# Attention, soft mixture of experts and MLP on one core: RoPE's last additions of pairs 1 to 5 as accumulating transfers from GpSimd's queue, with a new order of the first pairs

## The chip, the core and the metric

The kernel runs on one core of a Trainium2 chip. The core has a matmul engine (TensorE, PE in the rows), VectorE (DVE), ScalarE (ACT), GpSimd (POOL) and SyncE (SP), each with a queue of its own that it works off in order, and 16 DMA engines that all queues share. The metric is the device time of one execution in microseconds. The kernel before takes 566.4 us, the median of three runs (566.14 to 568.69).

## What is computed

The reference has three stages, all in float32:

- Attention over 4 batches of 8 heads, 576 positions, head size 64. Queries and keys are first rotated (RoPE): with the halves x1, x2 of a head's 64 numbers, the result is x1·cos - x2·sin and x1·sin + x2·cos. Then come the scores (scaled by 1/8), their softmax and the product with the values.
- A soft mixture of experts on the 2304 tokens of width 512: logits against `phi` (32 slots), a softmax over tokens that mixes tokens into slots, 8 experts of 4 slots each with a hidden width of 1024 and ReLU, and a softmax over slots that mixes the experts' results back into tokens.
- An MLP from 512 to 2048 and back, with the squared ReLU between.

```
q_rot, k_rot = (rotate(q), rotate(k))
scores = scale * np.matmul(q_rot, k_rot.transpose(0, 1, 3, 2))
attn = np.exp(scores - max);  attn = attn / (sum + 1e-09)
out = np.matmul(attn, v)
```

The host lays out the inputs. For each pair of heads it gives one array `qk[p]` of 128 rows (two heads of 64) by four planes of 576 columns: keys, queries, keys with their halves swapped, queries with their halves swapped. With that, RoPE is plain arithmetic on whole rows: plane · cos + swapped plane · (signed) sin.

## The kernel before

**The work in pairs.** The 32 heads are worked off as 16 pairs, 0 to 15. A pair passes through these steps (the function names are those of the listing):

- `load` brings the four planes into one of two buffers, `raws[p % 2]`, 1152 KB, from SyncE's queue. From pair 4 on a load is cut into three pieces. A buffer can be loaded again once `parts_pair` of the pair that held it is through.
- `rope_pair` computes in place, for each half t (0: keys, 1: queries): plane t times cos (d = 0), plane t + 2 times sin (d = 1), and the addition of the second to the first (d = 2). Each is one operation on 128 x 576 numbers. For pair 0 it runs on VectorE, for all other pairs on GpSimd (L543, a helper line that all of them share).
- `parts_pair` splits each rotated plane into a high part, rounded to the matmul's format by ScalarE (L577), and a low part, the difference, by GpSimd (L543 again, into tLa or tLb). Three products of high and low parts replace one exact product.
- `windows` copies the last 64 columns of the parts on ScalarE.
- `max_unit` computes scores from the high parts alone on TensorE (L654) and takes row maxima on VectorE (L665), nine units a pair (four blocks of 128 keys for each of two query halves, and one unit, called BOTH, for the keys left over, for both query halves together). `max_rows` turns the maxima into rows, which two small transfers (L703, 2.5 KB each) carry to where `st_unit` reads them.
- `st_unit` computes the scores (L738, six matmuls) less the maxima (L745, two matmuls) into one of three pairs of score banks, ScalarE takes the exponential (L758), and GpSimd adds the first two blocks of a half into one partial sum (L766; in the last two pairs also further blocks, L771, listed by `folded`).
- `pv_unit` multiplies with the values (L789; L784 for BOTH). `norm` sums the exponentials with matmuls against ones (L813) and scales on VectorE. `logits` (L863, L868) and transposes (L886) pass the result on; after every fourth pair `slots_in` mixes the tokens into slots (L931, L969).

Filler matmuls (L1880) stand where the plan expects TensorE to wait.

**The order.** The kernel doesn't run these functions in their order. `Plan.op` records each operation with its engine, what it reads and writes, and a rank; `emit` then lays them out one after the other, always the one of lowest rank among those that can start soonest by the plan's estimates of durations. The ranks stand in the table `ORDER`, by function and engine: the first number in a row is the first operation of that kind recorded, and so on through the pairs. In `("rope_pair", "POOL", None)` of the kernel before, six numbers belong to a pair: 35, 41, 49 are the two multiplications and the addition of pair 1's keys, 45, 54, 68 those of its queries. In `("parts_pair", ...)` two numbers belong to a pair, in `("max_unit", ...)` and `("st_unit", ...)` nine, in the order of `SEQ`: four blocks of the first query half, BOTH, four of the second; in `("st_unit", "POOL", None)` two partial sums a pair. Ranks of one table can be compared across engines: a lower rank is planned earlier. Each engine then takes its own operations strictly in the order of emission, and semaphores hold one back until what it reads is there.

The place of the change is `rope_pair`:

```
(0, a, a, None, ALU.mult, tk[0], ka),
(1, b, b, None, ALU.mult, tk[1], kb),
(2, a, a, b, ALU.add, kb, ka),
```

In `norm`, the matmuls against ones write four quarters of 32 rows, so that up to four run beside each other; pairs of quarters are added later on VectorE. With four operands (the partial sum, blocks 2 and 3, BOTH) or two, all quarters are in use. Only the last pair's second half has three.

**After attention** the expert weights (`free`, L1174) are loaded into the buffers that attention has left, then the experts and the MLP run, the MLP's second product at L1806.

Of the kernel before, what the change touches and what calls it, by code (L numbers as in the profile page):

```python
# [15 lines left out]
ALU = mybir.AluOpType  # L16
# [22 lines left out]
class Plan:  # L39
# [23 lines left out]
            11, 12, 15, 13, 16, 18  # L63
# [5 lines left out]
            17, 19, 55, 79, 117, 150, 194, 224, 273, 305, 346, 361, 429, 454, 526, 531, 631, 633, 721, 724, 815, 818, 910, 914, 1013, 1015, 1101, 1104, 1193,  # L69
            1196, 1261, 1268  # L70
        ),
        ("parts_pair", "POOL", None): (
            22, 28, 60, 86, 124, 160, 199, 230, 279, 314, 359, 369, 435, 460, 532, 543, 637, 648, 732, 742, 825, 836, 922, 929, 1023, 1032, 1112, 1120, 1202,
            1210, 1273, 1281
        ),
        ("rope_pair", "POOL", None): (
# [4 lines left out]
        ),  # L81
        ("load", "SP", None): (
            36, 99, 173, 176, 180, 237, 240, 242, 322, 323, 327, 373, 377, 379, 468, 471, 473, 557, 561, 565, 659, 662, 665, 753, 755, 758, 846, 849, 852, 942,
            946, 949, 1043, 1045, 1047, 1131, 1133, 1136
        ),
        ("windows", "ACT", None): (
            23, 30, 82, 81, 156, 132, 226, 217, 309, 296, 406, 408, 499, 502, 606, 608, 698, 701, 791, 794, 884, 887, 988, 990, 1078, 1081, 1168, 1171, 1265,
            1275, 1331, 1332
        ),
# [7 lines left out]
        ),  # L97
        ("max_unit", "DVE", None): (
# [13 lines left out]
        ),  # L112
        ("max_rows", "SP", None): (
            51, 62, 134, 136, 219, 222, 312, 317, 415, 417, 509, 510, 615, 618, 707, 710, 800, 803, 893, 896, 997, 1000, 1087, 1090, 1177, 1180, 1270, 1274, 1358,
            1355, 1422, 1418
        ),
        ("max_rows", "ACT", None): (
            52, 63
# [1853 lines left out]
```

## Time and profile before

| | |
|---|---|
| median of three runs | 566.4 us |
| the profiled execution's own time | 565.09 us |
| its span, first to last instruction | 563.3 us |
| TensorE busy | 544.0 us (97%) |
| VectorE busy | 398.6 us (71%) |
| ScalarE busy | 295.7 us (52%) |
| GpSimd busy | 229.9 us (41%) |
| granted TensorE clock | 1.0 throughout |
| read from and written to device memory | 77.92 and 6.82 MB |

The profile comes from one execution under the hardware profiler. Times in it count from the first instruction. The attention stage lasts until about 294 us, the experts until about 335, the MLP to the end. A share of busy time is a mean over these stages: GpSimd's 41% is near 100% in the first 110 us and nothing after attention. Busy times of TensorE include overlapping matmuls, whose ends are modelled, so its work is better read from how far apart the starts of equal units lie. In a timeline row, the brackets give the time the engine stood idle before the row, and what ended it.

### The profile page before, as it was taken

To read this page: it belongs to the slowest core of one execution; us is meant where nothing else is said; L and a number is where in the kernel's file an instruction comes from. 1 tells how busy PE (TensorE), PEld (TensorE's weight loads), DVE (VectorE), ACT (ScalarE), POOL (GpSimd) and SP (SyncE) were. 2 spreads that over 40 slices of the span, in tenths; PEclk is the share of its full clock that TensorE was granted. 3 is DMA by queue.
4 is the path that set the end of the run, shared out by engine and by line. 5 is a ranking of instruction groups with operands and counts; after the bars stand their busy time and mean duration, and the time that the engine had idled before them with its cause. 6 is when DMAs were issued, how large, how long until landed. Compare 5 with 4: busy or idle time off the path is not lost.

```text
span 563.3 us, 13271 instructions
## 1 busy us (share of the span) xinstructions
PE 544.0 (97%) x5406; PEld 416.7 (74%) x5406; DVE 398.6 (71%) x878; ACT 295.7 (52%) x568; POOL 229.9 (41%) x178
## 2 busy tenths in 40 slices
PE   4999999999999999999999999999999999999996
PEld 3656666566665666666642258999999999999996
DVE  6587788888897887876468748965775595554553
ACT  2334545664555655544426548975944564354440
POOL 4999999988889788723610000000000000000000
PEclk9999999999999999999999999999999999999999
DMA  7447796877784357222989997132200220000333
GB/s 237 139 132 184 167 249 188 221 192 195 210 219 117 93 144 201 100 99 101 338 295 396 409 401 255 39 111 76 76 1 1 76 76 2 1 1 1 113 113 112
DMA packets 37741, 85.68 MB, mean 152 GB/s; under 512 B 12176, under 2 KB 12848, under 8 KB 36528
## 3 DMA queue, kind: packets, MB, share of 16 engines
q1 hardware_dynamic: 37398, 84.24, 48.3%
q8 instruction: 42, 0.69, 0.5%
q10 hardware_dynamic: 282, 0.59, 0.4%
q14 instruction: 19, 0.16, 0.1%
HBM read 77.92 MB, written 6.82 MB: 150 GB/s over the span
## 4 chain that ended last, share of the span: by engine, by line
PE 81%; DMA 9%; DVE 5%; POOL 2%; ACT 1%; issue 1%; SPq 0%; DVEq 0%
PE bank L1806 35%; PE bank L738 11%; PE obank L789 11%; PE bank L654 5%; PE bank L813 5%; PE bank L745 3%; PE obank L1736 3%; DVE mcol L665 2%; DMA w__1345<-in_w_dram 2%; DMA tEb<-in_w_dram 2%; DMA tLb<-in_w_in_dram 2%; PE obank L784 2%; PE bank L886 2%; DMA ident<-in_ident_dram 1%; POOL arena L543 1%; DMA w__448<-in_w_dram 1%
## 5 line engine op out<-in xcount | busy, mean ns | idle before, releaser
L758 ACT ACTIVATE tO<-bank 128x576 f32<-128x576 f32 x140 | 84.2, 650 | 84.4 <-PE bank L745 83.3
L665 DVE TENSOR_REDUCE mcol<-bank 128x2 f32<-128x576 f32 x144 | 103.2, 749 | 22.6 <-PE bank L654 13.1
L543 POOL TENSOR_TENSOR arena<-arena 128x576 f32<-128x576 f32 x78 | 111.0, 1444 | 8.8 <-DMA arena<-in_qk_dram 8.0
L1806 PE MATMUL bank<-w,tEb 128*128 128x256 f32 x864 | 106.5, 279 | 0.1
L1806 PEld LDWEIGHTS bank<-w,tEb 128*128 128x128 f32 x864 | 103.5, 188 | 2.4 <-issue 1.6
L789 PE MATMUL obank<-tO,pb 128*64 128x288 f32 x496 | 74.8, 419 | 0.0
L766 POOL TENSOR_TENSOR pb<-tO 128x576 f32<-128x576 f32 x30 | 42.9, 1430 | 31.0 <-ACT tO L758 29.4
L1806 PE MATMUL bank<-w,tEa 128*128 128x256 f32 x432 | 53.0, 278 | 0.0
L1806 PEld LDWEIGHTS bank<-w,tEa 128*128 128x128 f32 x432 | 51.6, 188 | 1.2 <-issue 1.2
L1806 PE MATMUL bank<-w,tO 128*128 128x256 f32 x432 | 51.6, 277 | 0.0
L1806 PEld LDWEIGHTS bank<-w,tO 128*128 128x128 f32 x432 | 51.1, 188 | 0.0
L789 PEld LDWEIGHTS obank<-tO,pb 128*64 128x64 f32 x496 | 29.8, 136 | 22.7 <-issue 9.3
L1747 ACT ACTIVATE pb<-obank 128x384 f32<-128x384 f32 x47 | 21.7, 495 | 36.8 <-PE obank L1736 36.8
L1747 ACT ACTIVATE w__1091<-obank 128x384 f32<-128x384 f32 x48 | 21.8, 491 | 36.5 <-PE obank L1736 36.2
L654 PEld LDWEIGHTS bank<-tEb 64*128 64x128 f32 x180 | 16.3, 184 | 21.5 <-DVE mcol L665 4.4
L813 PE MATMUL bank<-tO,ones 128*32 128x288 f32 x224 | 31.9, 409 | 0.0
L654 PE MATMUL bank<-tEb 64*128 64x288 f32 x180 | 30.5, 355 | 0.7 <-DVE mcol L665 0.5
L819 DVE STREAM_TRANSPOSE bank<-bank 128x288 f32<-128x288 f32 x32 | 15.9, 496 | 19.2 <-PE bank L813 15.8
L543 POOL TENSOR_TENSOR tLb<-arena,tEb 128x576 fp32r<-128x576 f32 x20 | 28.6, 1448 | 1.3 <-ACT tEb L577 1.3
L738 PE MATMUL bank<-tEb 64*128 64x288 f32 x180 | 28.5, 313 | 0.3 <-DVE mcol L665 0.2
L1736 PE MATMUL obank<-x,tO 128*128 128x384 f32 x95 | 26.8, 336 | 0.5 <-DVE tO L1664 0.5
L738 PE MATMUL bank<-tLb,tEb 64*128 64x288 f32 x180 | 26.6, 292 | 0.0
(299 smaller groups left out, 1095.2 us busy)
## 6 DMA issues: line engine op xcount, KB each, us to landing
arena<-in_qk_dram SPq DMA_DIRECT2D x14, 576.0 KB
arena<-in_qk_dram SPq DMA_DIRECT2D x12, 512.0 KB
arena<-in_w_dram SPq DMA_DIRECT2D x8, 512.0 KB
pb<-in_v_dram SPq DMA_DIRECT2D x12, 320.0 KB
arena<-in_qk_dram SPq DMA_DIRECT2D x3, 1152.0 KB
tLb<-in_w_in_dram SPq DMA_DIRECT2D x3, 1024.0 KB
pb<-in_w_in_dram SPq DMA_DIRECT2D x3, 1024.0 KB
w__448<-in_w_dram SPq DMA_DIRECT2D x4, 512.0 KB
```

The costliest lines, as they stand in the source:

```text
L543: ENG[e].tensor_tensor(out=o, in0=x, in1=y, op=how)
L654: nc.tensor.matmul(on_ring(tok)[:, j, 0:HQ], lhsT=x[rows], rhs=hi[rows, 0, HALF[c]], start=(u < BOTH or c == 0), stop=(u < BOTH or c == 1),)
L665: lambda e: nc.vector.tensor_reduce(out=mcol[:, h, :, u], in_=on_ring(tok)[:, :, 0:HQ], op=ALU.max, axis=AX.X),
L738: nc.tensor.matmul(st[:, j, 0:HQ], lhsT=w[rows], rhs=q[y][rows, HALF[c]], start=(i == 0 and (u < BOTH or c == 0)), stop=False,)
L745: nc.tensor.matmul(st[:, j, 0:HQ], lhsT=pick[rows, w : w + 128], rhs=mrow[rows, HALF[c]], start=False, stop=(u < BOTH or c == 1),)
L758: lambda e: nc.scalar.activation(out=pr, in_=on_ring(tok)[:, :, 0:HQ], func=AF.Exp, scale=0.125),
L766: lambda e: nc.gpsimd.tensor_tensor(out=acc, in0=one, in1=pr, op=ALU.add),
L789: nc.tensor.matmul(BANKS[6 + h][o, 0:HQ], lhsT=vr[:, u, j, :], rhs=pr[:, j, :], start=(h == 0 and u == 0), stop=(h == 1 and u == 3))
L813: nc.tensor.matmul(sm[QUAD[2 * j + w], 0:HQ], lhsT=one, rhs=x[:, j, :], start=(i == 0), stop=(i + w + 2 > last))
L1736: lambda e, i=i, t0=t0: nc.tensor.matmul(BANKS[i][:, 0:384], lhsT=wst_of()[:, 128 * fc : 128 * fc + 128], rhs=cst_of()[:, t0 : t0 + 384], ...
L1747: lambda e, i=i, h=h: nc.scalar.activation(out=rg_of()[:, 0, h], in_=BANKS[i][:, 0:384], func=AF.Relu),
L1806: nc.tensor.matmul(BANKS[c][:, cols], lhsT=gt[:, x, 128 * c : 128 * c + 128], rhs=wo[:, fc % 2, y, cols], start=(fc % FQ == 0 and i == 0 a ...
```

## The change

- For pairs 1 to 5 (`MOVED`) `rope_pair` records only the two multiplications of each half. One operation follows them: a DMA issued from GpSimd's queue that reads planes 2 and 3 of the buffer and adds them to planes 0 and 1 in place (`accum_op=ALU.add`), for keys and queries at once: 128 rows of 1152 numbers, 590 KB. Ten additions go and five DMAs come. Its rank is the fifth number of a pair in `("rope_pair", "POOL", None)`.
- The ranks of pairs 0 to 5 are new on all engines. From about pair 6 on, each rank is the old one less 5, so the order there is the same.
- In pair 0 (VectorE) the addition of the first half goes behind the second multiplication of the second half.
- `folded` reads a table `FOLDED` in place of its condition. `norm` spreads an odd last operand over two quarters, half of the columns each.

```
         ("rope_pair", "DVE", None): (
-            11, 12, 15, 13, 16, 18
+            11, 12, 16, 13, 15, 17
...
         ("parts_pair", "ACT", None): (
-            17, 19, 55, 79, 117, 150, 194, 224, 273, 305, 346, 361, 429, 454, 526, 531, 631, 633, 721, 724, 815, 818, 910, 914, 1013, 1015, 1101, 1104, 1193,
...
+            18, 19, 82, 79, 130, 134, 220, 216, 273, 279, 377, 372, 429, 436, 519, 532, 625, 628, 716, 719, 810, 813, 905, 909, 1008, 1010, 1096, 1099, 1188,
...
         ("parts_pair", "POOL", None): (
-            22, 28, 60, 86, 124, 160, 199, 230, 279, 314, 359, 369, 435, 460, 532, 543, 637, 648, 732, 742, 825, 836, 922, 929, 1023, 1032, 1112, 1120, 1202,
...
+            21, 28, 112, 101, 135, 141, 250, 238, 280, 286, 398, 391, 435, 440, 549, 538, 634, 646, 727, 737, 820, 831, 917, 924, 1018, 1027, 1107, 1115, 1197,
...
         ("rope_pair", "POOL", None): (
-            35, 41, 49, 45, 54, 68, 76, 96, 110, 116, 131, 143, 149, 171, 186, 193, 207, 214, 236, 244, 262, 250, 285, 295, 290, 304, 330, 336, 341, 352, 381,
...
+            45, 49, 35, 40, 54, 76, 92, 60, 68, 109, 158, 166, 150, 175, 187, 199, 205, 213, 219, 244, 314, 335, 320, 326, 343, 355, 365, 380, 348, 405, 416, 454,
...
         ("max_unit", "PE", "r"): (
-            21, 24, 25, 29, 32, 34, 38, 40, 42, 92, 94, 103, 84, 85, 100, 107, 111, 113, 162, 175, 185, 165, 167, 182, 189, 192, 196, 227, 243, 269, 229, 241,
-            265, 277, 278, 286, 310, 340, 360, 324, 326, 355, 365, 375, 385, 372, 432, 450, 400, 419, 446, 456, 466, 478, 464, 529, 551, 493, 513, 542, 560, 576,
...
+            25, 22, 32, 24, 38, 29, 34, 41, 43, 107, 87, 93, 113, 118, 116, 106, 102, 96, 145, 143, 206, 182, 155, 189, 168, 193, 197, 235, 255, 308, 233, 237,
+            274, 266, 272, 245, 291, 283, 347, 374, 337, 336, 371, 367, 316, 385, 389, 388, 379, 421, 426, 485, 472, 483, 482, 516, 498, 442, 520, 471, 554, 570,
...
         ("st_unit", "PE", "r"): (
-            64, 61, 70, 67, 77, 121, 115, 119, 125, 154, 151, 187, 178, 197, 206, 200, 203, 209, 257, 251, 276, 261, 288, 307, 292, 303, 337, 348, 345, 362, 351,
...
+            58, 66, 71, 63, 110, 119, 81, 84, 99, 172, 179, 164, 177, 159, 198, 190, 201, 203, 252, 248, 263, 259, 303, 300, 293, 295, 318, 357, 353, 361, 364,
...
         ("st_unit", "POOL", None): (
-            104, 138, 179, 223, 272, 321, 371, 410, 452, 508, 553, 612, 656, 700, 751, 793, 844, 886, 940, 992, 1042, 1080, 1129, 1170, 1217, 1263, 1301, 1340,
...
+            83, 126, 192, 227, 262, 305, 373, 427, 470, 528, 558, 602, 653, 695, 746, 788, 839, 881, 935, 987, 1037, 1075, 1124, 1165, 1212, 1258, 1296, 1335,
...
+    MOVED = (1, 2, 3, 4, 5)
+
     def rope_pair(p, g):
...
                 (2, a, a, b, ALU.add, kb, ka),
-            ):
+            )[: 2 if p in MOVED else 3]:
...
+        if p in MOVED:
+            op(
+                {"POOL": 1.0}, lambda e: nc.gpsimd.dma_start(out=raws[i][:, 0:2, :], in_=raws[i][:, 2:4, :], accum_op=ALU.add), g + 5,
+                [("raw", i, n, s) for n in (2, 3) for s in range(3)], [("raw", i, n, s) for n in (0, 1) for s in range(3)], kb=590,
+            )
...
+    FOLDED = {NP - 2: ((2, 3), (2, 3)), NP - 1: ((2, 3), (2,))}
+
     def folded(p, h):
 
-        return () if p not in LATE else (2,) if (p, h) == (NP - 1, 1) else (2, 3)
+        return FOLDED.get(p, ((), ()))[h]
...
             for i in range(0, len(things), 2):
                 for j in range(2):
-                    for w in range(min(2, len(things) - i)):
-                        x, _ = things[i + w]
-                        one = half_ones[:, h] if i + w == (3 if last == 3 else 1) else ones[:, 0:32]
+                    for w in range(2):
+                        x, k = things[min(i + w, last)]
+                        one = half_ones[:, h] if k == both else ones[:, 0:32]
+                        cols = slice(0, HQ) if i + 1 <= last else slice(0, HQ // 2) if w == 0 else slice(HQ // 2, HQ)
                         nc.tensor.matmul(
-                            sm[QUAD[2 * j + w], 0:HQ], lhsT=one, rhs=x[:, j, :], start=(i == 0), stop=(i + w + 2 > last)
+                            sm[QUAD[2 * j + w], cols], lhsT=one, rhs=x[:, j, cols], start=(i == 0), stop=(i + 2 > last)
                         )
```

## Rows read from the trace of the kernel before

**Rows 1.** The page: GB/s moved in each of 40 slices of 14.1 us.

```profile
GB/s 237 139 132 184 167 249 188 221 192 195 210 219 117 93 144 201 100 99 101 338 295 396 409 401 255 39 111 76 76 1 1 76 76 2 1 1 1 113 113 112
```

**Rows 2.** Stretches: length; PE, PEld, DVE, ACT, POOL busy; clock, DMA share, GB/s.

```profile
30.03:52.57 22.54, 21.66 (x250) 14.14 (x248) 16.60 (x42) 11.34 (x21) 22.46 (x17) 1.00 0.60 170
52.57:67.44 14.87, 14.74 (x158) 9.47 (x159) 12.15 (x33) 6.66 (x14) 14.87 (x12) 1.00 0.79 174
...
100.19:118.89 18.70, 18.38 (x217) 11.30 (x219) 16.51 (x39) 10.52 (x25) 16.21 (x12) 1.00 0.86 216
...
135.04:151.18 16.14, 16.14 (x198) 10.74 (x201) 13.41 (x33) 9.53 (x20) 14.04 (x10) 1.00 0.78 209
...
167.38:185.28 17.90, 17.90 (x216) 11.25 (x218) 14.49 (x38) 11.13 (x27) 14.06 (x10) 1.00 0.63 145
```

**Rows 3.** Timeline of TensorE, first half: start, duration, line, tiles, shapes, count.

```profile
22.51 0.44 PE L738 MATMUL bank<-tEa 64*128 64x288 f32 x2
...
23.47 0.44 PE L738 MATMUL bank<-tEa 64*128 64x288 f32 x2
...
47.65 0.29 PE L738 MATMUL bank<-tEb 64*128 64x288 f32 x2
...
48.19 0.29 PE L738 MATMUL bank<-tEb 64*128 64x288 f32 x2
```

**Rows 4.** The chain of waits, merged: start, duration, what.

```profile
253.17 0.70 PE bank L886 x5
253.97 2.08 PE bank L813 x32
...
269.21 3.70 DMA tEa<-mrow
...
276.15 1.12 PE obank L789 x8
...
283.44 1.12 PE bank L813 x12
```

**Rows 5.** Stretches, max matmuls (L654) alone: PE, PEld, clock, DMA share, GB/s.

```profile
20.43:30.03 9.60, 2.15 (x14) 1.25 (x14) 1.00 0.47 108
30.03:52.57 22.54, 4.56 (x32) 2.51 (x30) 1.00 0.60 170
...
135.04:151.18 16.14, 3.15 (x20) 1.72 (x20) 1.00 0.78 209
```

**Rows 6.** Stretches, score matmuls (L738) alone, same columns.

```profile
20.43:30.03 9.60, 4.84 (x36) 4.00 (x36) 1.00 0.47 108
30.03:52.57 22.54, 8.12 (x84) 6.13 (x84) 1.00 0.60 170
52.57:67.44 14.87, 5.18 (x54) 3.93 (x54) 1.00 0.79 174
...
135.04:151.18 16.14, 5.37 (x60) 4.45 (x60) 1.00 0.78 209
```

**Rows 7.** Timeline of GpSimd.

```profile
13.48 4.12 POOL L543 TENSOR_TENSOR arena<-arena,w__132 128x576 f32<-128x576 f32 x3
...
119.22 1.41 POOL L543 TENSOR_TENSOR arena<-arena 128x576 f32<-128x576 f32 x1 [2.67 <-DMA arena<-in_qk_dram]
```

**Rows 8.** Timeline of SyncE's queue: start, time to issue, line, transfer, count.

```profile
13.54 0.33 SPq L528 DMA_DIRECT2D arena<-in_qk_dram  x1
...
109.54 1.84 SPq L535 DMA_DIRECT2D arena<-in_qk_dram  x3
```

**Rows 9.** Row maxima: ns min/median/max of one, first and last start.

```profile
L703 ACTq DMA_DIRECT2D tEb<-mrow x2: 595/935/1275, 18.5 to 21.2; - x2
```

**Rows 10.** Stretches in the columns of rows 2, cut finer.

```profile
19.00:21.00 2.00, 1.43 (x8) 0.92 (x9) 1.39 (x5) 0.68 (x1) 1.69 (x2) 1.00 0.01 2
...
75.00:78.00 3.00, 3.00 (x36) 1.60 (x38) 2.18 (x3) 2.13 (x4) 3.00 (x3) 1.00 1.07 306
```

**Rows 11.** Timeline of ScalarE.

```profile
38.22 0.68 ACT L577 ACTIVATE tEb<-arena 128x576 fp32r<-128x576 f32 x1 [3.32 <-POOL arena L543]
```

More of the change, by code (lines that the diff above doesn't have):

```diff
@@ L85 @@
+            941, 944, 1038, 1040, 1042, 1126, 1128, 1131
         ),
         ("windows", "ACT", None): (
-            23, 30, 82, 81, 156, 132, 226, 217, 309, 296, 406, 408, 499, 502, 606, 608, 698, 701, 791, 794, 884, 887, 988, 990, 1078, 1081, 1168, 1171, 1265,
-            1275, 1331, 1332
+            23, 30, 89, 121, 137, 142, 226, 261, 312, 310, 386, 417, 478, 479, 600, 603, 693, 696, 786, 789, 879, 882, 983, 985, 1073, 1076, 1163, 1166, 1260,
+            1270, 1326, 1327
         ),
         ("max_unit", "PE", "r"): (
[6 rows of a table removed]
[6 rows of a table added]
@@ L115 @@
-            1355, 1422, 1418
+            51, 61, 140, 146, 232, 236, 338, 334, 411, 403, 513, 511, 609, 612, 702, 705, 795, 798, 888, 891, 992, 995, 1082, 1085, 1172, 1175, 1265, 1269, 1353,
+            1350, 1417, 1413
         ),
         ("max_rows", "ACT", None): (
-            52, 63
+            52, 62
         ),
         ("<lambda>", "SP", None): (
-            65,
+            80,
         ),
         ("natural_table", "SP", None): (
-            71, 74, 78
+            73, 98, 64
         ),
@@ L174 @@
+            1372, 1445, 1438, 1435, 1442, 1406, 1411, 1503, 1505, 1471, 1475, 1495, 1494, 1500, 1498
         ),
         ("logits", "PE", "q"): (
-            220, 318, 411, 504, 611, 704, 797, 890, 994, 1084, 1174, 1267, 1360, 1417, 1478, 1502
+            210, 306, 401, 507, 606, 699, 792, 885, 989, 1079, 1169, 1262, 1355, 1412, 1473, 1497
         ),
         ("logits", "DVE", None): (
-            225, 320, 416, 505, 616, 708, 801, 894, 998, 1088, 1178, 1272, 1364, 1423, 1483, 1506
+            214, 309, 409, 512, 610, 703, 796, 889, 993, 1083, 1173, 1267, 1359, 1418, 1478, 1501
@@ L187 @@
+            1487, 1489, 1504, 1512
         ),
         ("prepare", "SP", None): (
-            390, 517, 483, 604, 589, 669, 684, 789, 775, 855, 870, 986, 971, 1050, 1064, 1166
+            382, 468, 473, 598, 584, 664, 679, 784, 770, 850, 865, 981, 966, 1045, 1059, 1161
         ),
         ("prepare", "ACT", None): (
-            431, 436, 463, 549, 556, 570, 619, 624, 653, 728, 745, 757, 808, 822, 839, 932, 938, 953, 1002, 1006, 1034, 1108, 1123, 1135
+            408, 402, 424, 537, 527, 561, 614, 618, 648, 723, 740, 752, 803, 817, 834, 927, 933, 948, 997, 1001, 1029, 1103, 1118, 1130
@@ L193 @@
         ),
         ("prepare", "DVE", None): (
[L195 removed]
+            420, 434, 551, 592, 641, 660, 733, 778, 827, 846, 946, 974, 1022, 1041, 1111, 1155
         ),
         ("slots_in", "DVE", None): (
[L198 removed]
+            515, 539, 544, 565, 893, 931, 934, 950, 1271, 1403, 1408, 1427, 1502, 1515, 1518, 1523, 1524
@@ L199 @@
         ),
         ("slots_in", "ACT", None): (
-            520, 528, 535, 902, 905, 913, 918, 1282, 1280, 1285, 1287, 1511, 1515, 1513, 1518
+            525, 523, 542, 897, 900, 908, 913, 1277, 1275, 1280, 1282, 1506, 1510, 1508, 1513
         ),
         ("slots_in", "PE", "f"): (
-            548, 550, 931, 933, 1404, 1405, 1516, 1519
+            533, 534, 926, 928, 1399, 1400, 1511, 1514
         ),
         ("slots_in", "PE", "q"): (
-            566, 569, 948, 952, 1424, 1426, 1522, 1527
+            560, 563, 943, 947, 1419, 1421, 1517, 1522
@@ L208 @@
         ),
         (None, "PE", None): {
-            0: 1512, 1: 1521
+            0: 1507, 1: 1516
         },
         (None, "DVE", None): {
-            0: 1514, 1: 1524, 2: 1526
+            0: 1509, 1: 1519, 2: 1521
         },
         (None, "ACT", None): {
-            0: 1525
+            0: 1520
         },
@@ L799, in norm @@
         things = [(accs[n], ("acc", n)), *(p_slot(p, h, u) for u in (2, 3, BOTH) if u not in folded(p, h))]
+        both = p_slot(p, h, BOTH)[1]
         last = len(things) - 1
@@ L809, in sums @@
                 for j in range(2):
-                    for w in range(min(2, len(things) - i)):
-                        x, _ = things[i + w]
-                        one = half_ones[:, h] if i + w == (3 if last == 3 else 1) else ones[:, 0:32]
+                    for w in range(2):
+                        x, k = things[min(i + w, last)]
+                        one = half_ones[:, h] if k == both else ones[:, 0:32]
+                        cols = slice(0, HQ) if i + 1 <= last else slice(0, HQ // 2) if w == 0 else slice(HQ // 2, HQ)
                         nc.tensor.matmul(
-                            sm[QUAD[2 * j + w], 0:HQ], lhsT=one, rhs=x[:, j, :], start=(i == 0), stop=(i + w + 2 > last)
+                            sm[QUAD[2 * j + w], cols], lhsT=one, rhs=x[:, j, cols], start=(i == 0), stop=(i + 2 > last)
                         )
-        op({"PE": 0.97 if last > 1 else 0.49}, sums, g + T["sums"], [k for _, k in things], [("sm", n)], take="ring", tok=tok, mode="q")
+        op({"PE": (0.49, 0.73, 0.97)[last - 1]}, sums, g + T["sums"], [k for _, k in things], [("sm", n)], take="ring", tok=tok, mode="q")
         op(
```

36 lines of the change are left out of this document (15 added, 21 removed), and 67 rows, old and new, of the table ORDER.

## The prediction

> **What bounds the kernel now.** I read the page first, then the stretches of the attention part, then TensorE's instructions by line, and last GpSimd, ScalarE and the transfers around the first pairs. The page's bytes per slice [rows 1] show that in slices 20 to 24, from 268 to 338 us, 295 to 409 GB/s flow: expert weights, which can be loaded only as attention frees their slots. So what attention gains or loses goes through to the end.
>
> The stretches [rows 2] are cut at the starts of the matmuls that take the rows left over from both query halves (L784), once a pair. From 30 to 67 us GpSimd is full: 22.46 of 22.54 us, 14.87 of 14.87. That is what the change relieves. But a pair takes 16.14 us (135.04 to 151.18) with GpSimd idle for 2 us of it, so there TensorE sets the pace and not GpSimd. The question is how much TensorE time the first pairs lose at all.
>
> I price the work of the early stretches by undisturbed work. A score unit (six matmuls of L738, two of L745) takes 0.54 us (47.65 to 48.19 [rows 3]); 16 sums 1.04, half of 2.08; a value product 0.56; a pair's transposes 0.70 [rows 4]; a max matmul 0.16, as 3.15 / 20 [rows 5].
> - 30.03 to 52.57: 84 matmuls of L738 against 60 [rows 6], so 4 units more (2.1); 12 max matmuls more [rows 5] (1.9); 16 sums more (1.0); no transposes (-0.7), one row step more (0.2). 16.1 + 4.5 = 20.6 against 22.54: 1.9 lost.
> - 52.57 to 67.44: one unit less (-0.5), 16 sums less (-1.0), no logits (-0.4, my estimate from their 16 small matmuls); with these the count falls from 198 to 158 [rows 2]. 14.2 against 14.87: 0.7 lost.
> - 20.43 to 30.03: 6 units (3.2), 4 value products (2.2), 14 max matmuls (2.2): 7.6 against 9.60: 2.0 lost. Of these 1.7 are four units at 0.96 instead of 0.54 (22.51 to 23.47 [rows 3]); the granted clock column says 1.00 there too, and these units stay where they are. 0.3 remains.
> - 100.19 to 118.89 against the other stretch with slot work, 167.38 to 185.28 [rows 2]: 18.70 - 17.90 = 0.8.
>
> Together 3.7 us. That is the most that a better order and a freer GpSimd can return to the bound engine; what is taken from GpSimd itself is not the gain.
>
> **The change, part by part.** *Removed:* ten additions on GpSimd, each 4.12 / 3 = 1.37 us [rows 7]: 13.7 us. *Added on GpSimd:* five DMA issues. No row shows GpSimd issuing. Bounds: 0.33 us (SyncE's issue of 1152 KB [rows 8]) and 1.27 (the longer of ScalarE's two [rows 9]). I take that row's median, 0.94, since ScalarE too issues from a queue that computes. GpSimd keeps 13.7 - 4.7 = 9 us.
>
> *Added as a wait:* the sum is ready not at the end of an instruction but when the transfer lands, and both halves (k and q) come at once. Behind it wait ScalarE's two rounded copies (L577, about 0.7 each), queued among the exponentials, and TensorE's first max matmul of that pair, which holds back all matmuls behind it. The latency L, from the start of the issue to the landing, is the unknown. Below: 3.70 us, the row maxima of 2.5 KB [rows 4], nearly all fixed cost. Above: a later pair's load, issued from 109.54 on [rows 8], is what GpSimd waits for until 119.22 [rows 7]: 9.7 us, beside other loads. Nearest in bytes is pair 2's load, 1152 KB issued at 13.54 [rows 8] and over by 19.0, for from then on the transfers are still, share 0.01 [rows 10]: at most 5.4 us. The accumulation has 590 KB to read from each of two places, 1180 KB. With 0.94 for 0.33 us of issue L is 6.0, alone; nearer 8 where loads run beside it.
>
> The Trainium skill, "Collectives: The Full Stack", section "The bandwidth ceiling: the fold count and why AG ≠ RS ≠ AR", says that an addition on the way is not itself slow, but needs two source reads on the ring that is the bottleneck, and so runs at half the rate of a copy. No row here shows an addition in a transfer. If one reading counted instead, L would be about 4.8, nothing would come late, and the sum below would be -2.2.
>
> *Where it is needed.* I follow the new order along GpSimd's queue. Pair 1's four multiplications start at 13.5 [rows 7], so the issue is at 19.0. TensorE does four units to 24.4, two value products and two units (2.2), and wants pair 1 at 26.6; less two copies (1.4) L may be 6.2. Pair 2: three multiplications, one partial sum, a multiplication and a low part from 19.9, issue at 28.1; TensorE, through 9 max units of pair 1 (VectorE at 0.7 each) and the rest of pair 0, comes to it at 36.5: L up to 7.0. Pair 3: two operations, then the low parts of pair 2, which wait for its landing (34.2 to 36.9), four multiplications, issue at 42.4, wanted at 52.5: 8.7. Pair 4: issue at 53.0, wanted at 61: 6.6. Pair 5: its multiplications stand behind pair 2's second partial sum (about 64.5), issue at 71.4, wanted at 79: 6.2. So alone the transfers come just in time. Pairs 4 and 5 run beside loads (75 to 78 us: share 1.07 [rows 10]); at L of 8 pair 5 is 1.8 late, pair 4 1.4. A delay of TensorE is also slack for the next pair, so I don't add them up: 1.0, between 0 and 3.5.
>
> *What comes back.* Pair 2's second copy waits for GpSimd until 38.22 [rows 11]; now it could be there by 35.5, and three max units of pair 2 stand before pair 1's first score unit. That works on the 1.9 us of the stretch from 30 us. The other losses stand beside VectorE's work as much as GpSimd's. I take 2.0 of the 3.7: -2.0, between 0 and -3.7.
>
> *Order of pair 0 on VectorE:* the first half's addition goes one place back, the second's stays, and the maxima need both: 0. If that cover failed, one operation of 0.7 us. *Sums of the last pair's second half:* the odd operand is split over the idle quarters, so the last third of the 1.12 us from 283.44 [rows 4] halves: -0.2, on the chain. The folding table gives the same units as before: 0. More transfers, 5 x 590 KB, lie beside loads that GpSimd waits for seldom: 0 here, in L above.
>
> Sum: -2.0 + 1.0 - 0.2 = -1.2 us on the profiled execution's 565.1 us (563.3 of span and 1.8 around it): 563.9. The median of the three runs, 566.4, is 1.3 above the profiled one, so I forecast 566.4 - 1.2 = **565.2 us**: no change within 0.5% (2.8 us), which is about what a measurement can tell from none.
>
> **The rivals.**
> - *Most of TensorE's loss comes back* (L at 5 to 6 even beside loads): -3.0 to -3.9, about 562.8. For it: GpSimd is full exactly where the loss is. Against: VectorE's 9 maxima and the normalisation of pair 0 fall into the same stretch, and stay. 0.28.
> - *The sum arrives late* (slower): L decides, from about 6.2 on. At 9.7 pairs 1, 4 and 5 are 3.5, 3.1 and 3.5 late; ScalarE stands, the score banks fill, TensorE stops. One lateness carried on gives +3.5; where GpSimd's low parts and so the next issue are late too, twice that. Less the gain of 1.2 to 2: +2 to +6, about 570. For it: the share in rows 10 from 75 us, and no spare in the places above. Against: pair 1's transfer runs when the others are still. 0.20.
> - *The issue is dear*: GpSimd held 3 us for each transfer, so that 13.7 us of additions become 15 of issue, pairs 2 to 5 are issued as late as they were added before, and the latency comes on top: +3, 569.4. For it: no row shows a GpSimd issue; against: both bounds above. 0.07. The Trainium skill, "SBUF — State Buffer", section "SBUF: two separate sides", says that a DMA from GpSimd's queue gets no descriptors written while VectorE holds the port that they share. By that an issue would be held for one VectorE operation, 0.75 us at most here; no row of before shows it.
> - *It does nothing for the bound engine*: gain and lateness both nil, only the sums: 566.2. 0.03.
>
> **How the numbers follow.** Forecast 0.42; with the last rival, no change has 0.45. Faster by over 0.5%: 0.28. Slower: 0.20 + 0.07 = 0.27. The range 562.0 to 570.8 takes in the first rival (down to -3.9, and 0.5 for the spread of runs) and the lower two thirds of the second; the forecast's own range is 563.6 to 567.5.
>
> **What would show it.** Right: the landings at most 6.5 us after the start of the issue; GpSimd with idle time from 30 to 84 us; the L784 matmuls of pair 6 at 133 to 135 instead of 135.04; the later distances unchanged (16.14). Wrong: ScalarE's L577 or TensorE's L654 waiting for a DMA in the first 90 us, above all before pairs 4 and 5; more than 2 us on GpSimd from an issue to the next operation; pair 6 at 132 or earlier, or after 137.

## The result, and the profile after

The changed kernel takes 573.27 us (median of 4 runs, 572.51 to 574.32) against 566.27 of the kernel before on the same chip: ratio 1.0117, 95% interval 1.0083 to 1.0150. The forecast was 565.2, no change; it is 7 us slower. The profiled run has a span of 571.7 us against 563.3, 8.4 more.

The expert weights' transfers, which follow attention, moved with it; the page's GB/s of the changed kernel answer to [rows 1], slices 20 to 24 (215 336 378 409 402 against 338 295 396 409 401; a slice is now 14.3 us):

```profile
GB/s 234 168 202 189 226 241 87 235 226 189 207 218 127 142 162 126 173 98 98 215 336 378 409 402 259 65 148 75 75 1 1 75 75 1 1 2 1 111 112 110
```

Then the stretches of the changed kernel, cut as in [rows 2] at the starts of the matmuls on the rows left over (now L793), pairs 0 to 6:

```profile
34.57:51.90 17.33, 17.20 (x195) 10.74 (x194) 13.95 (x40) 7.35 (x13) 16.41 (x13) 1.00 0.96 232
51.90:70.76 18.86, 17.26 (x198) 11.05 (x196) 13.95 (x33) 8.64 (x18) 11.48 (x10) 1.00 0.85 195
70.76:93.95 23.19, 19.56 (x189) 11.62 (x188) 15.15 (x43) 7.99 (x15) 18.57 (x14) 0.85 0.65 160
93.95:109.07 15.12, 15.12 (x172) 10.44 (x170) 12.21 (x27) 8.92 (x19) 12.45 (x9) 1.00 0.90 205
109.07:126.56 17.49, 16.95 (x203) 10.50 (x201) 13.69 (x36) 9.38 (x21) 15.90 (x12) 1.00 0.82 229
126.56:142.73 16.17, 16.17 (x196) 10.75 (x195) 13.89 (x33) 9.50 (x19) 14.48 (x10) 1.00 0.76 202
```

Up to pair 1 nothing is lost: 51.90 against 52.57. Pair 2 is 3.4 us late (67.37 before, the first of its matmuls; [rows 2] cuts at the second, 67.44), pair 3 10.0 (83.90), pair 6 7.8 (134.97), and the later distances are 16.14 to 16.17 as they were. The loss arises between 52 and 94 us and goes through to the end.

GpSimd is no longer full (11.48 of 18.86), which was the aim, and TensorE now waits, which it hardly did: length less busy time is 0.13 + 1.60 + 3.63 + 0 + 0.54 = 5.9 us from 34.57 to 126.56. Before, [rows 2] give 0.88 + 0.13 + 0.32 = 1.3, and the two stretches between them nothing:

```profile
67.37:83.90 16.53, 16.53 (x197) 10.89 (x196) 12.98 (x33) 6.96 (x14) 16.45 (x13) 1.00 0.86 214
83.90:100.12 16.22, 16.22 (x196) 10.72 (x195) 13.88 (x35) 9.91 (x19) 16.21 (x12) 1.00 0.72 189
```

In the third stretch of the changed kernel the granted clock is 0.85 besides. In two-microsecond slices:

```profile
82.00:84.00 2.00, 0.90 (x14) 0.66 (x10) 1.14 (x2) 0.00 (x0) 2.00 (x3) 1.00 1.02 383
84.00:86.00 2.00, 0.64 (x4) 0.39 (x6) 0.00 (x0) 1.95 (x4) 2.00 (x3) 0.77 0.82 319
86.00:88.00 2.00, 2.00 (x10) 0.93 (x10) 1.23 (x3) 1.22 (x3) 2.00 (x2) 0.50 0.02 7
88.00:90.00 2.00, 2.00 (x10) 0.77 (x8) 1.80 (x3) 0.13 (x1) 1.92 (x3) 0.50 0.02 4
90.00:92.00 2.00, 2.00 (x19) 0.75 (x21) 0.55 (x2) 0.00 (x0) 0.96 (x1) 0.52 0.04 8
92.00:94.00 2.00, 2.00 (x44) 1.56 (x36) 1.47 (x8) 0.51 (x1) 0.00 (x0) 1.00 0.20 42
```

After an idle 2.5 us TensorE runs at 0.50, the lower level of 1.2 GHz, from about 85 to 92. The same stretch of tiny_transfer (an experiment below), also 189 matmuls but all at 1.00, is busy for less:

```profile
69.35:87.82 18.47, 16.97 (x189) 10.86 (x187) 15.04 (x43) 8.10 (x15) 17.87 (x14) 1.00 0.57 154
```

19.56 - 16.97: the low clock costs 2.6, by this one pair of stretches. Idle time (4.6 more) and clock (2.6) make 7.2 of the 8.4 us.

TensorE's three longest waits from 20 to 128 us (total, times, longest):

```profile
PE bank L661 <- ACT tEb L584: 2.5, 1, 2.5
PE bank L754 <- DMA tEa<-mrow: 1.2, 1, 1.2
PE bank L661 <- ACT tEa L584: 1.1, 1, 1.1
```

The first is pair 5's rounded copy, the third pair 3's: the late sums. The second is the row maxima of pair 3. How pair 5 comes to be late stands in the queues. GpSimd, ScalarE and SyncE of the changed kernel (`arena` holds the buffers of q and k; `arena<-arena` is the accumulating DMA, `arena<-in_qk_dram` a pair's load):

```profile
35.80 2.79 POOL L542 TENSOR_TENSOR tLb<-arena,tEb 128x576 fp32r<-128x576 f32 x2 [0.32 <-ACT tEb L584]
38.90 5.56 POOL L542 TENSOR_TENSOR arena<-arena,w__132 128x576 f32<-128x576 f32 x4 [0.30 <-DMA arena<-in_qk_dram]
44.76 0.88 POOL L574 DMA_DIRECT2D arena<-arena  x1 [0.30 <-POOL arena L542]
...
55.78 1.75 POOL L542 TENSOR_TENSOR tLa<-arena,tEa 128x576 fp32r<-128x576 f32 x1
...
67.94 1.41 POOL L775 TENSOR_TENSOR pb<-tO 128x576 f32<-128x576 f32 x1 [3.40 <-ACT tO L767]
70.53 5.52 POOL L542 TENSOR_TENSOR arena<-arena 128x576 f32<-128x576 f32 x4 [1.18 <-DMA arena<-in_qk_dram]
76.35 0.88 POOL L574 DMA_DIRECT2D arena<-arena  x1 [0.30 <-POOL arena L542]
```

```profile
53.02 1.26 ACT L584 ACTIVATE tEa<-arena 128x576 fp32r<-128x576 f32 x2 [3.89 <-DMA arena<-arena]
...
65.58 1.88 ACT L767 ACTIVATE tO<-bank 128x576 f32<-128x576 f32 x3 [3.34 <-PE bank L754]
...
84.05 1.26 ACT L584 ACTIVATE tEb<-arena 128x576 fp32r<-128x576 f32 x2 [2.77 <-POOL pb L775]
```

```profile
60.57 1.22 SPq L534 DMA_DIRECT2D arena<-in_qk_dram  x2
...
64.56 1.78 SPq L534 DMA_DIRECT2D arena<-in_qk_dram  x3
73.04 1.49 SPq L710 DMA_DIRECT2D tEa<-mrow  x2
```

And SyncE of the kernel before, the same three steps (pair 5's load, pair 3's row maxima, pair 6's load):

```profile
53.45 1.83 SPq L535 DMA_DIRECT2D arena<-in_qk_dram  x3
...
66.93 1.51 SPq L703 DMA_DIRECT2D tEa<-mrow  x2
68.54 1.82 SPq L535 DMA_DIRECT2D arena<-in_qk_dram  x3
```

And the transfer of pair 3's sum, from the chain of waits:

```profile
44.76 8.24 DMA arena<-arena
```

Pair 3's multiplications are released by its load, but only 0.3 us after pair 2's low parts have left GpSimd; either would have held them until about then. Its sum lands at 53.0, its low parts end at 57.5 (before: 53.4), and only then is the buffer free for pair 5. SyncE, with v and w1 pieces ahead, issues that load at 60.6 instead of 53.45; it lands at 70.5, the sum is issued at 76.35, the copy starts at 84.05 and TensorE goes on at 85.36. (The releaser named on the copy's row, a partial sum on GpSimd, ended at the moment of the landing; in filler18 below the copy starts in the middle of that partial sum, released by the transfer.) So lateness was handed on in two ways: by the buffer to the pair after next, and by TensorE itself, whose late scores hold up the exponentials (65.58), and these GpSimd's partial sum at 67.94. At pair 5 the second is the larger: of the 5 us between the forecast issue (71.4) and the measured one, 3.4 lie ahead of that partial sum and 1.2 are the wait for the load behind it.

### The profile page after: what moved, and what is told of

Its sections match the earlier page's. It is cut to its first block, busy times and chain, and to the rows that moved or that the text cites. A ratio compares the mean times of both kernels' runs of the same rounds, so it can differ in the third digit from the quotient of the medians.

```text
span 571.7 us, 13291 instructions
## 1 busy us (share of the span) xinstructions
PE 546.5 (96%) x5410; PEld 417.6 (73%) x5410; DVE 397.7 (70%) x878; ACT 294.8 (52%) x568; POOL 220.5 (39%) x173
## 4 chain that ended last, share of the span: by engine, by line
PE 76%; DMA 11%; POOL 6%; DVE 3%; ACT 2%; issue 2%; SPq 0%; DVEq 0%; POOLq 0%
PE bank L1817 35%; PE obank L798 10%; PE bank L747 9%; PE bank L661 5%; PE bank L824 5%; DMA arena<-in_qk_dram 5%; POOL arena L542 4%; PE bank L754 3%; PE obank L1747 3%; DMA tEb<-in_w_dram 2%; DMA tLb<-in_w_in_dram 2%; PE obank L793 1%; DMA arena<-arena 1%; PE bank L897 1%; POOL tLb L542 1%
## 5 line engine op out<-in xcount | busy, mean ns | idle before, releaser
L542 POOL TENSOR_TENSOR arena<-arena 128x576 f32<-128x576 f32 x68 | 96.0, 1436 | 9.9 <-DMA arena<-in_qk_dram 9.1
L798 PE MATMUL obank<-tO,pb 128*64 128x288 f32 x496 | 76.4, 426 | 0.0
L747 PE MATMUL bank<-tEb,tLb 64*128 64x288 f32 x180 | 26.6, 292 | 0.0
```

What stands on the lines that cost most here:

```text
L542: ENG[e].tensor_tensor(out=o, in0=x, in1=y, op=how)
L747: nc.tensor.matmul(st[:, j, 0:HQ], lhsT=w[rows], rhs=q[y][rows, HALF[c]], start=(i == 0 and (u < BOTH or c == 0)), stop=False,)
L798: nc.tensor.matmul(BANKS[6 + h][o, 0:HQ], lhsT=vr[:, u, j, :], rhs=pr[:, j, :], start=(h == 0 and u == 0), stop=(h == 1 and u == 3))
```

## The experiments

Ratios are to the kernel before, timed in the same set, with 95% intervals; microseconds lost or gained are each against the kernel before of that set. Theory 1 is that the latency of the transfers, added up over the pairs, is the loss; theory 2 that the new order is, above all by freeing pair 5's buffer late; theory 3 that it is SyncE's order. Theories 4 to 6 are stated in the expectations that use them.

### Sums left out, in the new order and in the old

```
-                {"POOL": 1.0}, lambda e: nc.gpsimd.dma_start(out=raws[i][:, 0:2, :], ...
+                {"POOL": 1.0}, lambda e: None, ...        # no_sum
...
+ d == 2 and 1 <= p <= 5 or tt(e, o, x, ...)               # no_sum_old_order
```

> The changed kernel, every queue in its order, with the five sums left out altogether (q and k of pairs 1 to 5 lack the second product): no issue, no transfer, no latency. Theory 4, the lateness of the sums is what stalls TensorE, at whatever place: idle from 20 us on 1.5 to 2 as before instead of 6.6, no low clock after 34, 563 to 566. Theory 5, the new order stalls it by itself, because rounded copies, loads and partial sums stand closer in it: idle 3 to 5, 568 to 571.

> The kernel before, every queue in its order, with the ten additions of pairs 1 to 5 left out: GpSimd is relieved of 13.7 us, at no cost anywhere. It is the most that the relief of GpSimd can bring. If GpSimd held up TensorE from 30 to 84 us, as the forecast has it: 1.5 to 3.7 us faster, 562.5 to 565. If TensorE's lost time there comes from VectorE or from the order of its own queue: 565.5 to 566.5, nothing to be had from the change even without its latency.

no_sum: 567.95 us, 1.0034 (1.0016 to 1.0052). no_sum_old_order: 566.15 us, 0.9993 (0.9970 to 1.0016). The second is the plainest answer of the study: 13.7 us of GpSimd taken away at no price gain nothing; its interval reaches down to -1.7 us, short of the -2.0 forecast. The first splits the loss: the new order costs 1.9 us with no sum in it, forming the sums in it the other 5.1 (7.0 - 1.9).

### The additions back in the new order, the DMAs in the old

```
-  nc.gpsimd.dma_start(out=raws[i][:, 0:2, :], in_=raws[i][:, 2:4, :], accum_op=ALU.add)
+  [tt('POOL', raws[i][:, t, :], raws[i][:, t, :], raws[i][:, t + 2, :], ALU.add) for t in range(2)]   # order_alone
...
+  the changed rope_pair in the kernel before, DMA at the rank of the second addition   # dma_alone
+  nc.gpsimd.dma_start(out=o, in_=y, accum_op=how) for each addition                    # split_alone
```

> The changed kernel with its order on all engines kept, instruction by instruction, but each of the five DMAs replaced at its place in GpSimd's queue by the pair's two additions (2 x 1.37 = 2.74 us of GpSimd against 0.88 of issue, and the sum is there 2.74 us after its start against 5.5 to 8.2). Theory 1, lateness that adds up: the sums are 2.7 to 5.4 us earlier in each pair, GpSimd has idle time for the 1.9 us more, so pair 5's matmuls of the rows left over are at 119 to 121 instead of 126.6, TensorE's clock stays at 1.00 from 85 to 92, and the time is 564 to 568. Rival, the new order of loads and exponentials itself is bad: pair 5 stays at 125 to 127 and the time at 571 to 574.

> The kernel before with the five accumulating DMAs in place of the ten additions, at the place of each pair's second addition; the order of loads, copies and matmuls as in the kernel before, except where a copy of the first half now has to stand behind the one transfer of both halves, and no change to the last pair's sums. Theory 2, the new order is what costs most: 565 to 569, the latency of 5 to 8 us in each pair covered in part by what GpSimd gains. Theory 1, the latency: both halves come 5 us after where the second came before, pairs 2 to 5 late each: 572 to 580.

> The kernel before, every engine's order kept, with each of the ten additions of pairs 1 to 5 replaced by an accumulating DMA of that half alone (288 KB, ten issues of 0.9 us instead of ten additions of 1.37). Each half's sum is there after its own latency, about 4 to 6 us against 1.37 before, and GpSimd's order, made for additions, has the low part one or two operations behind: GpSimd waits 2 to 3 us for each half. Theory 1 (latency): 575 to 590, the worst of all. Theory 2 (order): 566 to 570, since the order is the old one.

order_alone 573.06 us, 1.0106 (1.0081 to 1.0130); dma_alone 583.71, 1.0289 (1.0262 to 1.0316); split_alone 598.77, 1.0563 (1.0536 to 1.0590). Neither theory is right by itself. The old order with the DMA is the worst, past even the ranges of theory 1 (580 and 590), so theory 2, that the order costs most, fell; the new order is what makes the latency bearable. But order_alone, with no transfer of a sum in it, loses 7.0 us, as much as the changed kernel, where theory 1 expected 564 to 568: the loss can't be put down to the transfers' latency alone. In the new order the additions are no better than the DMAs: what they win in latency they lose in GpSimd's time. TensorE's waits in order_alone are others: a score bank held by an exponential that is queued on ScalarE behind pair 3's late low part, and a partial sum from GpSimd:

```profile
62.32 0.94 PE L661 MATMUL bank<-tEa 64*128 64x288 f32 x4 [1.76 <-ACT tO L767]
...
94.89 0.43 PE L824 MATMUL bank<-pb,ones 128*32 128x288 f32 x1 [1.83 <-POOL pb L775]
```

### What the latency is made of

```
+  nc.gpsimd.dma_start(out=raws[i][:, 0:2, :], in_=raws[i][:, 2:4, :])                               # plain_copy
+  nc.gpsimd.dma_start(out=raws[i][:, 0:2, 0:2], in_=raws[i][:, 2:4, 0:2], accum_op=ALU.add)         # tiny_transfer
```

> The changed kernel, but the five DMAs copy instead of accumulating: same queue, same bytes written, one source read per element instead of two (the addition is left out). It prices the accumulation. If the second read is what makes the transfer late: landing 1 to 2 us earlier (3.5 to 5 alone, 5 to 6 beside loads) and 566 to 570 us. If the latency is that of any transfer of this size from this queue: 5 to 8 us as before and 572 to 574.

> The changed kernel, but each accumulating DMA moves two of the 576 columns of each half: same issue and same waits, nearly no bytes (the rest of the sum is left out, so q and k of pairs 1 to 5 are not rotated fully). It prices the bytes. Theory 1 with a latency made mostly of bytes: issue to landing 2.5 to 4 us instead of 5.0 to 8.2, every sum 2 to 4 us earlier, 563 to 567 us. Rival, the order: 571 to 574 with the short latency. If the latency is mostly a fixed cost (landing still after 5 us): 570 to 573, and the bytes don't matter.

From start of the issue to landing, first the changed kernel, then plain_copy, then tiny_transfer:

```profile
DMA to landing us min/median/max: 5.0/6.2/8.2
```

```profile
DMA to landing us min/median/max: 3.2/3.6/5.8
```

```profile
DMA to landing us min/median/max: 2.6/4.5/6.3
```

plain_copy 570.78 us, 1.0076 (1.0046 to 1.0106); tiny_transfer 570.28, 1.0061 (1.0039 to 1.0084). By the medians a copy lands 2.6 us sooner than an accumulation of the same bytes, and that is worth 2.3 us of the whole (7.0 - 4.7). Against no sum (1.0034) even a copy or almost no bytes cost 2 to 3 us: the part that hardly any bytes still cost counts as much as the addition. The tiny transfer is not faster than the copy; its packets are more (1360 against 720).

### Pair 5: its load, its sum, a third buffer

```
+  lambda ...: p == 5 or QUEUE[q].dma_start(            # no_load5
-  36, 120, 156, 151, 154, 271, 268, 278, 292, ...
+  36, 120, 156, 151, 154, 246.1, 246.2, 246.3, 292, ...  # load5_early
+  ... accum_op=ALU.add) if p < 5 else [the two additions]   # adds_5; p < 3: adds_3to5
+  raws.append(x1 as [128, 4, S]); RB = [2 if p == 3 else p % 2 ...]   # spare_buffer
+  spare_buffer with the two additions for each DMA                    # spare_adds
```

> The changed kernel without the three transfers that load pair 5's q and k (60.6 to 63.1 in the changed kernel; pair 5 then computes on what is left in its buffer). Theory 2, the new order frees that buffer late: pair 3's low parts end at 57.5 instead of 53.4, the load goes out at 60.6 instead of 53.45 and is there at 70.5, and all of pair 5 hangs on it. Without the load pair 5's multiplications stand only behind the partial sum that ends at 69.4; that is 1.2 us earlier, and its issue at about 75, with fewer bytes beside it: TensorE idle 1 to 2 us less, the clock perhaps not lowered; 568 to 571 us. Theory 1, the accumulation's latency alone: pair 5's rounded copy is still at 83 or later and the time 572 to 574.

> The changed kernel with the three transfers of pair 5's load put ahead of the last v pieces of pair 3 and of a w1 load in SyncE's queue, so that only the free buffer holds them: out at 57.6 instead of 60.6. Theory 2: the load is there some 2 us earlier (68.5), but GpSimd's partial sum until 69.4 stands ahead of the multiplications, so pair 5 gains 1.1 us at most, and v comes later: 571.5 to 573. Theory 3, SyncE's order is what is wrong: 568 to 570.

> The changed kernel, its order kept, with pair 5's DMA alone replaced by the two additions on GpSimd (76.35 on, 2.74 us against a landing 7.6 us after the issue). Theory 2 with the late load: pair 5's rounded copy starts at 79 to 80 instead of 84, TensorE's idle of 2.5 us before pair 5 goes and the clock stays: 567 to 569. If GpSimd's 1.9 us more are late for pair 6 and the partial sum behind it: 570 to 572.

> The changed kernel, its order kept, with the DMAs of pairs 3, 4 and 5 replaced by additions on GpSimd, so that only pairs 1 and 2, whose transfers have little beside them, keep the DMA. Pair 3's sum at 47.5 instead of 53.0, so no wait of TensorE before 55; GpSimd 5.6 us more, of which it has idle 7 from 56 to 70. Theory 2: buffer 1 is still freed only behind pair 4's multiplications and the partial sum (59 instead of 57.5), pair 5's sum at 79 to 80: 567 to 570. If GpSimd is full again, so that the order and not the DMA is the loss: 572 to 574, as with all five.

> The changed kernel with a third buffer for the raw q and k: pair 3 is loaded into the rows x1 that hold the values of the second batch (written only from 110 us on), so its load need not wait for pair 1's low parts, and pair 5's load, which then takes pair 1's buffer, need not wait for pair 3's low parts; the planner orders the queues again by that. Everything else as in the changed kernel, the five accumulating DMAs too. Theory 2, the way over the buffer (late sum, late low part, late free, late load, late next sum) is the loss: issues of pairs 3 and 5 at 41 to 43 and below 71 instead of 44.8 and 76.35, no wait of TensorE over 1 us before 95, no low clock after 80: 563 to 567.5. Theory 1, the latency of each transfer by itself: what TensorE waits for pairs 3 and 5 shrinks by half at most, 569 to 573.

> The same third buffer and the same order, with each pair's two additions on GpSimd again at the place of the DMA. If with the loads freed the accumulating DMA is worth its 1.9 us of GpSimd a pair: this is 2 to 5 us slower than with the DMAs, 567 to 572. If the sum 3 to 5 us earlier is worth more: 1 to 3 us faster, 562 to 566.

| kernel | us | ratio | interval |
|---|---|---|---|
| no_load5 | 569.16 | 1.0050 | 1.0026 to 1.0073 |
| load5_early | 571.30 | 1.0091 | 1.0067 to 1.0114 |
| adds_5 | 572.66 | 1.0107 | 1.0077 to 1.0136 |
| adds_3to5 | 571.53 | 1.0088 | 1.0062 to 1.0115 |
| spare_buffer | 574.64 | 1.0134 | 1.0105 to 1.0163 |
| spare_adds | 571.94 | 1.0102 | 1.0075 to 1.0128 |

Only leaving the load out helps much, 4 us, within theory 2's range; but it brings pair 5's issue only from 76.35 to 74.90, and takes 1152 KB from beside the row maxima as well, whose wait is gone too, so it doesn't show how much of the 4 us is the late load. Every way that keeps all the work gives most of the time back elsewhere, or more. adds_5 (567 to 569 expected) has pair 3's rows left over at 90.21 instead of 93.95, and pair 4's at 109.03 against 109.07: GpSimd's longer work makes a partial sum 1.8 us late. load5_early, whose load goes out 1.3 us earlier (59.25), halves the waits for the copies, and TensorE waits 4.1 us for the row maxima instead. spare_buffer, where the planner also ordered the queues anew, frees pairs 3 and 5, but now pair 5's early load stands ahead of pair 4's, which goes out at 41.3 and lands at 51.9:

```profile
51.90 5.52 POOL L544 TENSOR_TENSOR arena<-arena 128x576 f32<-128x576 f32 x4 [3.75 <-DMA arena<-in_qk_dram]
```

```profile
68.35 0.61 PE L663 MATMUL bank<-tEb 64*128 64x288 f32 x2 [2.94 <-ACT tEb L586]
```

So pair 4 took pair 5's place in TensorE's wait, clock at 0.50 and all. My expectation of 563 to 567.5 was wrong: the buffer was one link, not the cause.

### Row maxima behind pair 6's load

In no_sum TensorE has one long wait, 3.4 us for pair 3's row maxima. Its chain (start, duration, what) and its stretches:

```profile
70.87 0.74 SPq L710
71.61 0.04 issue
71.66 6.32 DMA tEa<-mrow
77.98 0.04 issue
78.02 0.61 PE bank L754 x2
```

```profile
72.00:74.00 2.00, 2.00 (x18) 1.07 (x16) 1.86 (x8) 0.00 (x0) 2.00 (x3) 1.00 1.06 205
74.00:76.00 2.00, 0.62 (x8) 0.38 (x6) 1.96 (x4) 0.00 (x0) 0.76 (x1) 1.00 0.87 174
```

2.5 KB take 6.3 us while the DMA engines are busy throughout (share 1.06, at 205 GB/s). In the kernel before, whose SyncE sends them at 66.93, the transfers just then stand still:

```profile
66.00:68.00 2.00, 2.00 (x26) 1.40 (x26) 1.35 (x4) 1.88 (x4) 2.00 (x2) 1.00 0.02 3
```

So pair 6's load was moved behind them, on SyncE's queue alone:

```
+  (lambda issue=issue: behind_rows.append(issue)) if p == 6 else issue,   # load: kept back
...
+  len(rows_sent) == 2 and [behind_rows.pop(0)() for _ in range(len(behind_rows))],   # max_rows of pair 3: sent
```

> The changed kernel with the five sums left out, and with pair 6's load issued behind pair 3's row maxima on SyncE's queue, as in the kernel before, instead of ahead of them; every other order kept. In no_sum TensorE waited 3.4 us for those row maxima, 2.5 KB that took 6.3 us from their issue to the scores, while the loads of pairs 5 and 6 and of w1 kept the DMA share at 1.0. Theory 6, this place in SyncE's queue is what the new order costs by itself: no wait for the row maxima over 0.5 us, no low clock after 34, 565.5 to 567. Rival: pair 6's load, 8 us later, is late for GpSimd (its first multiplication at 78.5 in the changed kernel), which then holds up the partial sums and pair 5's low parts: 567.5 to 570.

> The changed kernel, its five accumulating DMAs included, with pair 5's load ahead of the v and w1 pieces (as in load5_early) and pair 6's load behind pair 3's row maxima. In load5_early TensorE waited 4.1 us for the row maxima. Theory 6 with theory 2: that wait goes, the waits for the rounded copies of pairs 3 and 5 of 0.8 us each stay, clock at 1.00 after 34: 567.5 to 570. Rival: pair 6's load is late for GpSimd or beside pair 5's transfer, and the time is given back: 571 to 573.

no_sum_load6_late 574.94 us, 1.0134 (1.0099 to 1.0169); loads_5_and_6 578.06, 1.0201 (1.0162 to 1.0240). The wait for the row maxima is gone in both, so what held them up is shown; and the rival came true, at a higher price than it gave: both times lie about 5 us past its ranges. GpSimd of no_sum_load6_late stands 6.7 us for pair 6's load, and the partial sum queued behind it reaches TensorE 3.9 us late:

```profile
80.92 4.11 POOL L546 TENSOR_TENSOR arena<-arena 128x576 f32<-128x576 f32 x3 [6.70 <-DMA arena<-in_qk_dram]
```

```profile
PE bank L832 <- POOL pb L783: 3.9, 1, 3.9
```

Neither place for pair 6's load is free. Which place of the new order costs its own 1.9 us stays open; one long wait is named, and taking it away alone doesn't pay.

### The clock, and the last pair's sums

```
+  if p == 5 and 5 not in filled:      # filler5: range(9), filler18: range(18)
+      filled.append(5)
+      for _ in range(9): nc.tensor.matmul(on_ring(tok)[:, 0, 384:512], lhsT=ident, rhs=ident, start=True, stop=True)
```

> The changed kernel with nine 128x128 matmuls of the identity put on TensorE just ahead of pair 5's first max matmul, into the unused columns of that unit's own bank; they run while TensorE waits for pair 5's rounded copy (82.8 to 85.4 in the changed kernel) and do nothing for the result. Theory 1's last term, the idle 2.5 us drops TensorE's clock to 0.50 for 6.5 us, which costs about 3 us: the clock stays at 1.00 from 85 to 92, pair 5's matmuls of the rows left over come 2 to 3 us earlier, at 124, time 570 to 571. Rival, the low clock stands beside other waits and costs nothing, or the fillers delay the wait by themselves: 572.5 to 574.

> The changed kernel with eighteen filling matmuls instead of nine ahead of pair 5's first max matmul, about 4.5 us, which is the whole wait of TensorE there. Theory 1's last term: with no idle time the clock stays at 1.00 from 85 to 92 and 2 to 3 us come back, less up to 1.5 by which the fillers outlast the wait: 571 to 572.5. Rival, the clock's loss is made up elsewhere: 573 to 575.

> The kernel before with nothing but the change to the sums of the last pair: eight matmuls of 288 columns, of which two become four of 144. The forecast's term: the sums on the chain take 0.94 instead of 1.12 us, -0.2; the time 566.0 to 566.6, not to be told from no change.

filler5 573.72 us, 1.0131 (1.0097 to 1.0164): the fillers took 2.27 us, the copy came later still, TensorE stood 2.1 us behind them and the clock fell. filler18 574.38, 1.0145 (1.0122 to 1.0168): the clock held after 86 us, but it had already been at 0.50 from 82 to 84, after the wait for the row maxima, and 4.29 us of fillers outlasted the copy. Neither prices the clock; the 2.6 us above, from two stretches with the same number of matmuls in two kernels, is the only measure of it.

sums_only (the kernel before with nothing but the diff's lines on the sums) 565.55 us, 0.9987 (0.9975 to 0.9999). The chain of sums_only, against 1.12 in [rows 4]:

```profile
283.44 0.91 PE bank L817 x16
```

It is the one version that is faster than the kernel before, by 0.5 us, with an interval that ends just short of no change (0.9999).

## Why the prediction was wrong

- **What bounds the kernel**: right. Attention's loss went through to the end (7.8 us at pair 6, 8.4 in the span).
- **GpSimd's prices**: right. The issue takes 0.86 to 1.01 us, forecast 0.94; the rival of a dear issue is out, and none of the five issues is longer than another by a VectorE operation (0.75 us). GpSimd got its idle time.
- **Latency L**: the size was right, 6 alone and 8 beside loads; 5.0 to 8.2 measured. Its place was not: pair 3's, taken as alone, took 8.2, and pair 4's, put beside loads, at most 5.8 (issue at 55.17, its copies start at 61.00 without a wait). The Trainium skill, "Collectives: The Full Stack", section "The bandwidth ceiling: the fold count and why AG ≠ RS ≠ AR", lays a reduction's half rate to two source reads; the copy's 3.6 and the accumulation's 6.2 us agree in direction, less than twofold, and no run here tells the second read from other costs of an addition. The Trainium skill, "DMA: Bandwidth & Descriptors", section "Anatomy of one DMA — SWDGE (gpsimd) path", has a fit of 2.0 us plus bytes over 436 GB/s; for 590 KB that makes an estimate of 3.4 us, which the copy's median of 3.6 bears out and the accumulation's 6.2 does not. The forecast's case of one reading (L about 4.8, nothing late, -2.2) was tried as plain_copy: the latency is as short, 3.2 to 5.8 us, but the time is 4.7 us longer than before, not 2.2 shorter.
- **What comes back, -2.0**: wrong; it is 0 (no_sum_old_order, 0.9993). I set TensorE's lost units beside a full GpSimd and took the one for the cause of the other. Only 1.3 us of TensorE's idle time was there to be had by [rows 2]; that the rest of my 3.7 was work placed elsewhere is my reading, no run shows it.
- **Lateness, "I don't add them up: 1.0"**: this is the step that failed most. Forming the sums in the new order costs 5.1 (no_sum against the changed kernel). Two errors are in it. The issue times were walked along GpSimd's queue with TensorE on time and each load in place: 19.0, 28.1, 42.4, 53.0, 71.4 against 19.5, 28.8, 44.8, 55.2, 76.35. At pair 5 it is the partial sum behind the late TensorE (3.4) and the load over the buffer that was freed late (1.2) that make the difference. And I wrote that a delay of TensorE is slack for the next pair; it is handed on instead, over the exponentials and over the buffer, and the idle time costs again in clock, a term that the sum didn't have (2.6). How much of the 5.1 goes each way stays open; nor is it the price of the latency alone, since the additions in the same order cost as much (order_alone).
- **The new order**: I had only a gain for it; by itself it costs 1.9. With the -2.0 that didn't come and 4.1 of lateness too little, that makes 8.0 of the 8.2 us between the forecast's -1.2 and the measured +7.0.
- **Sums, -0.2**: right on the chain, 1.12 to 0.91.
- The rival that came true is *the sum arrives late*, at about 570. Its rule (the next issue late too) was right; its place was right for pair 5 and wrong for pairs 1 and 4, where TensorE shows no such wait, while pair 3, which it didn't name, is late; its price was 3 us short.

## What to carry to other kernels

An engine that is full where another loses time is not yet its cause: leave its work out in an experiment, or look for a row in which the bound engine waits for it, before a gain is written into a sum. When work moves to a transfer, walk the whole ring: sum, its readers, the buffer they free, the load that waits for that buffer, the next sum; a latency that fits once may not fit the second time round. Where the transfers were busy throughout, one sent earlier made another late (pair 4's load in spare_buffer, the row maxima of 2.5 KB in load5_early).

## What the runs showed of the hardware that was not expected

- A 2.5 KB transfer took 6.3 us under other transfers (no_sum), against 3.70 in [rows 4].
- The DMA share stood at about 1.0 while 148 to 235 GB/s moved (the changed kernel at 64 us, and no_sum, which accumulates nothing, at 70; rows below), and 383 GB/s at the same share at 82 us: in these traces the share alone doesn't tell how much moves.

```profile
64.00:66.00 2.00, 2.00 (x26) 1.41 (x22) 1.86 (x9) 0.42 (x1) 0.54 (x1) 1.00 1.12 235
```

```profile
70.00:72.00 2.00, 2.00 (x26) 0.94 (x26) 1.94 (x7) 0.75 (x2) 2.00 (x3) 1.00 0.95 148
```

- An accumulation within SBUF of 590 KB lands after 5.0 to 8.2 us, a copy of the same after 3.2 to 5.8; one of 2 KB still after 2.6 to 6.3.
- TensorE fell to half its clock after idle spells of 2.5 us (the changed kernel) and 3.4 (no_sum), and ran 3 to 7 us at it. The length of the spell alone didn't decide: after one of 1.8 us in filler18 (to 79.25) it fell, after one of 1.95 in plain_copy (to 77.25) it stayed at 1.00 and the matmuls behind it 0.13 us apart.
- The clock column can miss a low clock. From 22 to 24 us the kernel before (column 1.00) and sums_only (column 0.50) start the same matmuls at the same pace, 0.24 us apart and 0.44 us long, against 0.13 and 0.29 from 26 us on. By their pace, the slow score units of [rows 3], which the prediction left unexplained because the column said 1.00, ran at the lower level too. First the kernel before, then sums_only:

```profile
22.00:24.00 2.00, 2.00 (x20) 2.00 (x20) 0.00 (x0) 1.41 (x3) 2.00 (x3) 1.00 0.27 50
```

```profile
22.00:24.00 2.00, 2.00 (x20) 2.00 (x18) 0.00 (x0) 1.41 (x3) 2.00 (x2) 0.50 0.33 62
```
